# Twelve of 56 gate-times-up products move from VectorE to GpSimd in a fused S4-convolution and gated-MLP kernel

## The chip, the cores and the metric

The kernel runs on one core of one Trainium2 chip. The metric is device time in microseconds (us) of that core. In the profile PE is TensorE (PEld its weight loads), DVE is VectorE, ACT is ScalarE, POOL is GpSimd and SP is SyncE. SBUF is the on-chip working memory, PSUM the memory into which matmuls accumulate. bf16 is the type of almost all data; matmuls accumulate in f32.

## The reference

Input `A_u` has 2048 tokens of 512 features. It is layer-normalised, and three things are summed:

```python
x  = A_u
xn = _layernorm(x)
return x + A(xn, ...) + B(xn, w_gate, w_up, w_down)

# A: a diagonal state-space (S4) layer with 128 modes: a kernel K of length 2048 per feature is
#    built from powers of exp(dt*A), the tokens are convolved with it, and xn*Dskip is added
# B: g = xn @ w_gate; u = xn @ w_up        (512 -> 1792)
#    h = sigmoid(g) * u
#    return h @ w_down                     (1792 -> 512)
```

The change touches only `h = sigmoid(g) * u`.

## The kernel before

**B, the gated MLP.** The 2048 tokens go in four groups of 512, the 1792 hidden features in 14 tiles of 128. Group `grp` and tile `k` make a unit, `un = 14*grp + k`, of 56. A unit is four matmuls of 128x512 for the gate (line 1031), four for up (line 1055), a sigmoid on ACT from PSUM into a slot of `hT_sb` in SBUF (line 1043, or 1046 for two units at once), and a product `hT = hT * up`, in place, on DVE (line 1070). The units in the list `UEV` (36 of 56) have their up result first copied by ACT from PSUM to one of the two slots of `us_sb` (line 1066), and the product then reads two SBUF operands. The other 20 products read up from PSUM. When the 14 products of a group are done, 4 x 14 matmuls with `w_down` follow (line 1099). For groups 0 to 2 their result goes to `glu_sb` and GpSimd issues a DMA that adds x to it (line 1136, six of them); the final sum is made on DVE at the end (line 1010).

**A, the convolution.** DVE squares a complex factor again and again (lines 679 and 681) and builds tables of powers, in four chunks of features, by complex multiplications of four `tensor_tensor` each (lines 737, 738, 742, 743) and by squarings that begin on ACT (line 790) and end on DVE (lines 795, 796). Matmuls turn the tables into the kernel K (lines 821, 841, 914). The tokens are transformed by matmuls (698, 892), multiplied with K's transform on DVE (919, 923) and transformed back (936, 995).

**GpSimd** has little: the `pow` of the layernorms (lines 482, 483, 499), two memsets of a table's first column per chunk (770, 771), a few prefix sums of four elements (712 to 716), the six DMAs of line 1136, and some memsets at the start.

**What sets the order.** Every step is registered with `pl.add(engine, cost, function, ...)`, with the slots that it takes (`acq`) and gives back (`rel`). A list written out in the file, `ORDER`, says in which order the steps are emitted; slots are handed out first-in-first-out in that same order. The costs and priorities of `pl.add` play no part while `ORDER` is there. Each engine runs its own instructions strictly in the order of emission and waits by semaphores on others. So the next copy into a `us_sb` slot (line 1066 on ACT) waits until the product that reads the slot is done, and the down matmuls wait for the products of their group.

Of the kernel before, what the change touches and what calls it, by code (L numbers as in the profile page):

```python
# [14 lines left out]
ALU = mybir.AluOpType  # L15
# [39 lines left out]
PPROD = 23.23  # L55
# [125 lines left out]
def _consts():  # L181
# [22 lines left out]
UEV = (3, 5, 8, 9, 10, 11, 15, 16, 17, 18, 19, 20, 21, 23, 24, 26, 27, 28, 29, 30, 31, 32, 33, 34, 35, 36, 37, 38, 39, 40, 41, 42, 43, 44, 45, 54)  # L204
ON_DVE = (64, 67, 73, 76, 97, 98, 110, 121, 122, 123, 124, 482, 836, 838)
ON_ACT = (2,)
ORDER = [
# [52 lines left out]
class _Plan:  # L260
# [32 lines left out]
    def run(self):  # L293

        for n in ORDER or range(len(self.ops)):
            op = self.ops[n]
# [24 lines left out]
def kernel(  # L321
# [12 lines left out]
    V, S, T, P, Y = nc.vector, nc.scalar, nc.tensor, nc.gpsimd, nc.sync  # L334
# [8 lines left out]
    pl = _Plan(dict(s=NS, gu=NGU, hT=NHT, zs=4, zx=2, xx=3, es=3, kb=2, pp=2, pq=2, vs=2, ot=3, tg=2, us=2, sq=2))  # L343
# [3 lines left out]
    def bank(slot, r=0):  # L347
        if slot.pool == "s":
            return pairs[slot.idx][:, 512 * r:512 * r + 512]
        return banks[slot.idx][:]  # L350

    def two(slot):
        return pairs[slot.idx][:]
# [14 lines left out]
    us_sb = const.tile([128, 2, 512], BF, name="us_sb")  # L368
# [85 lines left out]
    def w_at(w, cut, kt, k):  # L454
        n = max(n for n in range(len(cut) - 1) if cut[n] <= 128 * k)
        o = KT * cut[n] + kt * (cut[n + 1] - cut[n]) + 128 * k - cut[n]
        return w[:, o:o + 128]
# [19 lines left out]
    def ln_small(t0, t1, deps, prio):  # L477
# [7 lines left out]
        if t1 <= LN_ACT:  # L485
            def fv_():
                for i in range(t0, t1):
                    if i in ON_ACT:
                        V.scalar_tensor_tensor(out=stats[:, i % 4, 0:1], in0=mv[:, i, 0:1], scalar=-1.0, in1=mv[:, i, 0:1], op0=ALU.mult,
# [5 lines left out]
            def fw_():  # L495
                V.tensor_copy(out=q["m_f"], in_=mvb[:, s, 0])
            o_v = pl.add("DVE", 0.17 + 0.53 * len(set(range(t0, t1)) & set(ON_ACT)), fv_, deps, prio)
            o_w = pl.add("DVE", 0.14, fw_, [o_v], prio)
# [37 lines left out]
    def layernorm(i0, i1, prio):  # L536
        st = []
        for i in range(i0, i1):
            if i in ON_ACT:
                def fn(i=i):  # L540
                    S.activation(out=glu_sb[:, 7, :], in_=xn[:, i, :], func=ACT.Identity, scale=1.0 / D, accum_out=mv[:, i, 0:1])
                    S.activation(out=glu_sb[:, 7, :], in_=xn[:, i, :], func=ACT.Square, scale=float(D ** -0.5), accum_out=mv[:, i, 1:2])
# [206 lines left out]
    for c in range(4):  # L749
# [62 lines left out]
        for half_ in range(2):  # L812
            sl = _Slot("s")
# [63 lines left out]
    for p in range(NP):  # L877
        dsl = slice(DW * p, DW * p + DW)
        for u in UNITS[p]:
# [6 lines left out]
            sl = _Slot("s")  # L886
# [128 lines left out]
    for grp in range(4):  # L1015
        hts, prods = [], []
        for u2 in range(7):
            hs = _Slot("hT")
            hts.append(hs)
            evs = []  # L1020
            joint = grp == 0 and u2 in JOINT
            for k in (2 * u2, 2 * u2 + 1):
                a, b = _Slot("s" if joint else "gu"), _Slot("gu")
                if joint and k % 2:
                    a = a0
                a0 = a
                GP = 80 + grp + k * 0.01

                def fg(k=k, sl=a, w=wg_sb, grp=grp, c0=0, c1=512):
                    for kt in range(KT):  # L1030
                        T.matmul(bank(sl, k % 2)[:, c0:c1], w_at(w, CUT_G, kt, k), xnT[:, grp, kt, c0:c1], start=(kt == 0),  # L1031
                                 stop=(kt == KT - 1))
                if joint:
                    mg = pl.add("PE", 0.864, fg, xnT_ready[grp] + [l_wg[piece(k)]] + ([mg] if k % 2 else []), 80 + k * 0.001,
                                acq=[] if k % 2 else [a])
                elif grp == 0 and k < 3:
                    mg = pl.add("PE", 0.44, lambda fg=fg: fg(c1=256), [xnT_ready[0][0], l_wg[0]], 60 + k * 0.001, acq=[a])
                    mg = pl.add("PE", 0.44, lambda fg=fg: fg(c0=256), [xnT_ready[0][1], mg], 70 + k * 0.001)
                else:
                    mg = pl.add("PE", 0.864, fg, xnT_ready[grp] + [l_wg[piece(k)]], 80 + k * 0.001 if grp == 0 else GP, acq=[a])  # L1040

                def fs(k=k, sl=a, hs=hs):
                    S.activation(out=hT_sb[:, hs.idx, k % 2, :], in_=bank(sl), func=ACT.Sigmoid)  # L1043

                def fs2(sl=a, hs=hs):
                    S.activation(out=hT_sb[:, hs.idx, :, :].rearrange("p k n -> p (k n)"), in_=two(sl), func=ACT.Sigmoid)
                if joint:
                    es_ = pl.add("ACT", 0.90, fs2, [mg], PSIG, tab="sig", acq=[hs], rel=[a]) if k % 2 else None
                else:
                    es_ = pl.add("ACT", 0.48, fs, [mg] + evs[-1:], PSIG, tab="sig", acq=[hs] if k % 2 == 0 else [], rel=[a])  # L1050
                evs.append(es_)

                def fu(k=k, sl=b, grp=grp):
                    for kt in range(KT):
                        T.matmul(bank(sl), w_at(wu_sb, CUT_U, kt, k), xnT[:, grp, kt, :], start=(kt == 0),  # L1055
                                 stop=(kt == KT - 1))
                mu = pl.add("PE", 0.864, fu, xnT_ready[grp] + [l_wu[k // 7]], GP + 0.005, acq=[b])

                h = lambda hs=hs, k=k: hT_sb[:, hs.idx, k % 2, :]
                un = FT * grp + k  # L1060
                us = _Slot("us")
                on = un in UEV

                def feu(sl=b, us=us, on=on):
                    if on:
                        S.activation(out=us_sb[:, us.idx, :], in_=bank(sl), func=ACT.Identity)  # L1066
                eu = pl.add("ACT", 0.48, feu, [mu], PSIG, acq=[us] if on else [], rel=[b] if on else [], alt=(un, 1))

                def fpd(sl=b, h=h, us=us, on=on):
                    V.tensor_tensor(out=h(), in0=h(), in1=us_sb[:, us.idx, :] if on else bank(sl), op=ALU.mult)  # L1070
                tail = dict(rel=[us] if on else [b], alt=(un, 2))
                if joint and k % 2 == 0:
                    held = fpd, [eu, mu], tail
                    continue
                if joint:
                    prods.append(pl.add("DVE", 0.33, held[0], held[1] + [es_], PPROD, **held[2]))
                prods.append(pl.add("DVE", 0.33, fpd, [es_, eu, mu], PPROD, **tail))
        ges = []
        for jj in range(4):
            i = grp * 4 + jj  # L1080
# [114 lines left out]
```

## Time and profile before

| | |
|---|---|
| median of 3 runs | 223.22 us (221.82 to 225.51) |
| span of the profiled execution, first to last instruction | 219.8 us |
| what the median has around that span | 3.4 us |
| mean granted TensorE clock | 0.999 |
| products from SBUF on DVE (line 1070) | 36, shortest 394, median 424, longest 438 ns |
| products from PSUM on DVE (line 1070) | 20, shortest 656, median 684, longest 700 ns |
| copies of up to SBUF on ACT (line 1066) | 36, median 616 ns |
| GpSimd's longest group | line 714, 3 instructions, 6.1 us |

A duration of DVE or ACT in the profile overlaps the next instruction's by some 0.1 us; what an instruction takes from its engine is the time from its start to the next start. Lines are those of the kernel before. The two profiles' line numbers differ after line 206.

### The profile page before, as it was taken

Reading aid. Unit: us, or ns where it says so; the run is one execution under the profiler, and the core shown is the slowest. Engines: PE = TensorE matmul, PEld = TensorE weight load, DVE = VectorE, ACT = ScalarE, POOL = GpSimd, SP = SyncE. Lnnn points to the kernel's source line nnn. Section 1 sums busy time; section 2 is a strip of 40 time slices with the busy share of each in tenths; the row PEclk is TensorE's granted clock in tenths of the full one; section 3 lists DMA queues with packets and bytes.
Section 4 is the critical chain, followed back from the end, with each engine's and each line's share of the span. In section 5 each row is a group of like instructions: output and inputs, shape, how many; then the busy total and the mean of one; then the engine's idle time right before and its main releaser. Section 6 shows DMA issues by size and latency. Waiting matters only on the chain.

```text
span 219.8 us, 5357 instructions
## 1 busy us (share of the span) xinstructions
PE 209.2 (95%) x2075; PEld 105.0 (48%) x2103; DVE 202.2 (92%) x444; ACT 175.9 (80%) x283; POOL 22.6 (10%) x39
## 2 busy tenths in 40 slices
PE   7999988999999999999999999999989999999994
PEld 2544433444434454445555555554555455543453
DVE  3999999999999999999999999999989999993582
ACT  3699999999999999769899999977578978942000
POOL 2216001001000049100000004000020100000000
PEclk9999999999999999999999999999999999999999
DMA  5997069216667064526818579856857987688743
GB/s 172 333 425 298 7 180 317 80 42 143 237 134 206 18 198 97 202 82 178 244 55 237 152 244 210 212 173 169 228 111 236 265 265 232 189 234 209 220 158 136
DMA packets 40651, 41.36 MB, mean 188 GB/s; under 512 B 9009, under 2 KB 31922, under 8 KB 40498
## 3 DMA queue, kind: packets, MB, share of 16 engines
q1 hardware_dynamic: 39458, 39.12, 57.7%
q0 software_dynamic: 864, 1.57, 4.9%
q10 hardware_dynamic: 304, 0.33, 0.6%
q8 instruction: 16, 0.26, 0.5%
q14 instruction: 9, 0.07, 0.1%
HBM read 25.28 MB, written 12.06 MB: 170 GB/s over the span
## 4 chain that ended last, share of the span: by engine, by line
DVE 48%; PE 41%; DMA 4%; ACT 4%; issue 2%; POOL 0%; DVEq 0%; ACTq 0%
PE bank L1099 11%; DVE big L738 7%; PE pair L914 7%; DVE big L737 6%; PE bank L1031 6%; PE bank L1055 6%; DVE hT_sb L1070 6%; PE pair L936 5%; DVE stats L547 4%; DVE big L742 4%; DVE big L743 3%; DVE big L679 3%; DVE big L681 3%; DMA big<-c_E 3%; ACT big L290 3%; DVE big L613 2%
## 5 line engine op out<-in xcount | busy, mean ns | idle before, releaser
L290 ACT ACTIVATE big<-pair 128x1024 bf16<-128x1024 f32 (+2 forms) x75 | 73.4, 996 | 9.2 <-PE pair L936 1.9
L1055 PE MATMUL bank<-xnT,wu_sb 128*128 128x512 bf16 x214 | 54.4, 379 | 2.5 <-ACT us_sb L1066 1.3
L1031 PE MATMUL bank<-xnT,wg_sb 128*128 128x512 bf16 (+1 forms) x211 | 50.9, 367 | 1.4 <-ACT xnT L576 0.4
L1099 PE MATMUL bank<-wd_sb,hT_sb 128*128 128x512 bf16 (+1 forms) x230 | 50.2, 366 | 0.4
L1043 ACT ACTIVATE hT_sb<-bank 128x512 bf16<-128x512 f32 x52 | 32.1, 643 | 3.8 <-PE bank L1031 3.6
L1031 PEld LDWEIGHTS <-wg_sb 128*128 128x128 bf16 x236 | 21.9, 98 | 26.4 <-issue 5.2
L1099 PEld LDWEIGHTS <-hT_sb 128*128 128x128 bf16 x238 | 22.5, 98 | 24.8 <-issue 2.1
L1055 PEld LDWEIGHTS <-wu_sb 128*128 128x128 bf16 x224 | 21.0, 97 | 27.2 <-issue 5.4
L737 DVE TENSOR_TENSOR big<-big 128x1024 bf16<-128x1024 bf16 (+4 forms) x40 | 26.8, 670 | 0.1
L738 DVE TENSOR_TENSOR big<-big 128x1024 bf16<-128x1024 bf16 (+4 forms) x40 | 26.6, 666 | 0.0
L1066 ACT ACTIVATE us_sb<-bank 128x512 bf16<-128x512 f32 x36 | 22.4, 634 | 0.0
L919 DVE TENSOR_TENSOR big<-big 128x2048 bf16<-128x2048 bf16 x16 | 19.5, 1219 | 0.4
L914 PE MATMUL pair<-big 128*128 128x256 bf16 x160 | 19.8, 272 | 0.1
L914 PEld LDWEIGHTS <-big 128*128 128x128 bf16 x160 | 15.5, 98 | 4.9 <-issue 1.1
L790 ACT ACTIVATE sq_sb<-big 128x256 bf16<-128x256 bf16 (+2 forms) x20 | 13.7, 685 | 3.9 <-DVE big L743 3.8
L743 DVE TENSOR_TENSOR big<-big 128x512 bf16<-128x512 bf16 (+4 forms) x40 | 16.6, 414 | 0.0
L742 DVE TENSOR_TENSOR big<-big 128x512 bf16<-128x512 bf16 (+4 forms) x40 | 16.5, 413 | 0.0
L290 ACT ACTIVATE big<-big 128x256 bf16<-128x256 bf16 x36 | 15.7, 470 | 0.2
L1070 DVE TENSOR_TENSOR hT_sb<-hT_sb,us_sb 128x512 bf16<-128x512 bf16 x36 | 14.9, 421 | 0.0
L905 DVE COPY big<-big 32x1024 bf16<-32x1024 bf16 x32 | 13.5, 421 | 0.5
L1070 DVE TENSOR_TENSOR hT_sb<-hT_sb,bank 128x512 bf16<-128x512 bf16 x20 | 13.2, 684 | 0.5 <-PE bank L1055 0.5
L936 PE MATMUL pair<-big 64*64 64x512 bf16 (+1 forms) x256 | 12.8, 326 | 0.5 <-ACT big L290 0.2
(103 smaller groups left out, 222.2 us busy)
## 6 DMA issues: line engine op xcount, KB each, us to landing
big<-c_E SPq DMA_DIRECT2D x16, 320.0 KB, 4.4
z_scr<-big SPq DMA_DIRECT2D x16, 256.0 KB, 3.0
big<-z_scr SPq DMA_DIRECT2D x16, 256.0 KB, 3.5
v_scr<-big SPq DMA_DIRECT2D x16, 256.0 KB, 2.9
big<-in_A_u_dram SPq DMA_DIRECT2D x4, 512.0 KB, 8.5
big<-big SPq DMA_DIRECT2D x32, 64.0 KB, 3.1
big<-v_scr SPq DMA_DIRECT2D x4, 512.0 KB, 5.0
wu_sb<-in_B_w_up_dram SPq DMA_DIRECT2D x2, 896.0 KB
```

The source lines that it names most:

```text
L290: nc.scalar.activation(out=get(out), in_=get(in_), func=ACT.Identity)
L737: V.tensor_tensor(out=wide(outp), in0=wide(lo), in1=mre, op=ALU.mult)
L738: V.tensor_tensor(out=wide(tb()), in0=wide(lo), in1=mim, op=ALU.mult)
L742: V.tensor_tensor(out=outp[:, :, 0], in0=outp[:, :, 0], in1=tb()[:, :, 1], op=opr)
L743: V.tensor_tensor(out=outp[:, :, 1], in0=outp[:, :, 1], in1=tb()[:, :, 0], op=opi)
L914: T.matmul(two(sk)[:, o:o + DW], es()[:, g, kt, :], kT[p][:, kt, :], start=kt in (0, NKT - 1), stop=kt >= NKT - 2)
L936: T.matmul(two(sv)[o:o + 64, DW * (2 * g + y):2 * DW * (g + 1)], mab[b:b + 64, 2 * u + g, q, :], pq()[b:b + 64, q, ch] if y else pp()[b:b ...
L1031: T.matmul(bank(sl, k % 2)[:, c0:c1], w_at(w, CUT_G, kt, k), xnT[:, grp, kt, c0:c1], start=(kt == 0), stop=(kt == KT - 1))
L1043: S.activation(out=hT_sb[:, hs.idx, k % 2, :], in_=bank(sl), func=ACT.Sigmoid)
L1055: T.matmul(bank(sl), w_at(wu_sb, CUT_U, kt, k), xnT[:, grp, kt, :], start=(kt == 0), stop=(kt == KT - 1))
L1070: V.tensor_tensor(out=h(), in0=h(), in1=us_sb[:, us.idx, :] if on else bank(sl), op=ALU.mult)
L1099: T.matmul(bank(po)[:, 0:c[1] - c[0]], hT_sb[:, hts[k // 2].idx, k % 2, jj * 128:(jj + 1) * 128], wd_sb[:, k, c[0]:c[1]], start=first and ...
```

## The change

A new list names twelve units, all of them in `UEV`: one of group 0, seven of group 1, four of group 2. Their product is issued on GpSimd (`P`) and not on DVE (`V`). The copy of up to `us_sb` stays as it was, and `ORDER` is the same list, so PE, ACT and SP have the same instructions in the same order. DVE's sequence has the twelve products taken out. GpSimd's has them put in at the place where `ORDER` emits them. Of the waits, those that waited on DVE for one of the twelve products now wait on GpSimd.

```diff
 ON_ACT = (2,)
+ON_POOL = (11, 15, 16, 19, 20, 21, 23, 24, 28, 30, 32, 34)
...
-                on = un in UEV
+                pool = un in ON_POOL
+                on = un in UEV or pool
...
-                    V.tensor_tensor(out=h(), in0=h(), in1=us_sb[:, us.idx, :] if on else bank(sl), op=ALU.mult)
+                    (P if pool else V).tensor_tensor(out=h(), in0=h(), in1=us_sb[:, us.idx, :] if on else bank(sl), op=ALU.mult)
...
-                prods.append(pl.add("DVE", 0.33, fpd, [es_, eu, mu], PPROD, **tail))
+                prods.append(pl.add("POOL" if pool else "DVE", 1.4 if pool else 0.33, fpd, [es_, eu, mu], PPROD, **tail))
```

GpSimd's sequence after the third layernorm's `pow` (line 483) is now: products of units 11, 20, 23, 15; the first DMA of line 1136; products 24, 16, 21, 19; memsets (770, 771); the second DMA; the prefix sums (712 to 716); products 34, 30; memsets; products 28, 32; memsets; the other DMAs and line 861.

More of the change, by code (lines that the diff above doesn't have):

```diff
@@ L1067, with fpd @@
                 eu = pl.add("ACT", 0.48, feu, [mu], PSIG, acq=[us] if on else [], rel=[b] if on else [], alt=(un, 1))
-                def fpd(sl=b, h=h, us=us, on=on):
-                    V.tensor_tensor(out=h(), in0=h(), in1=us_sb[:, us.idx, :] if on else bank(sl), op=ALU.mult)
+                def fpd(sl=b, h=h, us=us, on=on, pool=pool):
+                    (P if pool else V).tensor_tensor(out=h(), in0=h(), in1=us_sb[:, us.idx, :] if on else bank(sl), op=ALU.mult)
                 tail = dict(rel=[us] if on else [b], alt=(un, 2))
```

## The prediction

> **What bounds the kernel now.** First the page, busy times and the slices over the span, then the chain that ended last:
>
> ```profile
> PE 209.2 (95%) x2075; PEld 105.0 (48%) x2103; DVE 202.2 (92%) x444; ACT 175.9 (80%) x283; POOL 22.6 (10%) x39
> ...
> PE   7999988999999999999999999999989999999994
> ...
> DVE  3999999999999999999999999999989999993582
> ACT  3699999999999999769899999977578978942000
> POOL 2216001001000049100000004000020100000000
> ...
> DVE 48%; PE 41%; DMA 4%; ACT 4%; issue 2%; POOL 0%; DVEq 0%; ACTq 0%
> ```
>
> PE and DVE are both full, and POOL looks free. Busy PE could hide slack, so I looked at its starts in the timeline: matmuls of 512 columns start 0.216 us apart through all of the middle, while the granted clock is 1.00. PE is full in fact. The windows view over the stretch that holds the products says how much a faster DVE could give:
>
> ```profile
> 40.00:200.00 160.00, 156.85 (x1788) 80.28 (x1811) 157.08 (x344) 140.83 (x225) 14.74 (x19) 1.00 0.63 176
> ```
>
> The columns are the length, then busy PE, PEld, DVE, ACT, POOL. PE is idle for 160.00 - 156.85 = 3.15 us there. Its order is fixed, so nothing that DVE gives up after 40 us can bring more than that. The other direction is open: in the ten-us windows from 40 to 150 DVE is busy 9.90 us or more, and the chain of waits stays on DVE without a break to about 108 us. Lost DVE time there has no reserve to go into.
>
> **What leaves DVE.** The groups view with shapes kept apart has the two kinds of product:
>
> ```profile
> L1070 DVE TENSOR_TENSOR hT_sb<-hT_sb,us_sb 128x512 bf16<-128x512 bf16 x36 | 14.9, 421 | 0.0
> ...
> L1070 DVE TENSOR_TENSOR hT_sb<-hT_sb,bank 128x512 bf16<-128x512 bf16 x20 | 13.2, 684 | 0.5 <-PE bank L1055 0.5
> ```
>
> All twelve are of the first kind. One starts at 79.22 and its follower at 79.56 in the timeline, another at 33.61 and 33.95: 0.338 us from start to start. DVE is relieved of 12 x 0.338 = 4.06 us.
>
> **What one product takes on GpSimd.** No row shows one. The nearest rows, from the timeline of POOL:
>
> ```profile
> 0.85 0.52 POOL L519 MEMSET glu_sb<- 128x512 bf16 x1
> ...
> 81.24 0.22 POOL L714 TENSOR_TENSOR pre<-pre,xnT 128x4 f32<-128x4 f32 x1
> ```
>
> The memset writes 512 elements per partition in 0.52 us; memsets of one element take 0.10. That is 0.42 us for a pass over 512 elements. A two-operand operation on nearly nothing costs 0.22. If both operands and the result pass side by side, the product takes 0.22 + 0.42 = 0.65; if one after another, 0.22 + 3 x 0.42 = 1.50. I take two passes for two operands, the write hidden: 0.22 + 2 x 0.43 = 1.08 us, the middle of the two ends.
>
> **Does GpSimd's latency hurt by itself?** I matched the copies of line 1066, the sigmoids and the products in the timeline to their units. On DVE a product starts up to 4 us after its inputs are there, since it queues. On GpSimd it starts when the copy ends. Inputs are ready at (us): unit 11 38.05; 20 57.45; 23 62.30; 15 66.26; 24 70.98; 16 74.20; 21 76.21; 19 79.64; 34 106.00; 30 110.82; 28 113.20; 32 127.93. The next copy into the same `us_sb` slot started at 42.45, 65.48, 68.33, 70.34, 73.53, 78.48, 78.98, 82.52, 112.56, 113.94, 117.92, 128.72. With 0.06 for the hand-over and 1.08 for the product, each is done 1.4 to 6.9 us ahead of that copy, but for unit 32, which is 0.35 late. The first down matmuls that need a moved product start at 43.69 (unit 11), 83.37 to 84.23 (15, 16, 19) and 139.0 (28, 32), all 2.7 us or more behind. Alone, then, the latency costs nothing until a product takes 1.08 + 1.4 = 2.5 us.
>
> What is queued behind the products on POOL waits longer: the first DMA of line 1136 goes from 50.32 to about 67.4 (unit 15), but its sum is read on DVE at 200 us; the memsets at 101.87 go to about 112 (unit 30), and the matmuls that read them run from 131.19; the prefix sums feed work near 196 us. These cost nothing. The third layernorm's `pow` stands ahead of unit 11 and keeps its place. No queue of SP or ACT is passed.
>
> **What GpSimd does to DVE.** This is the term that decides. DVE instructions that read two SBUF tensors fill its time: from 55 to 83 us all but three products from PSUM and one line-560 instruction, from 105 to 130 all but one of line 852. There is one place where GpSimd reads SBUF against that:
>
> ```profile
> 82.07 5.44 POOL L714 TENSOR_TENSOR pre<-pre,xnT 128x4 f32<-128x4 f32 x1
> ...
> 82.04 0.43 DVE L1070 TENSOR_TENSOR hT_sb<-hT_sb,us_sb 128x512 bf16<-128x512 bf16 x1
> 82.38 0.47 DVE L737 TENSOR_TENSOR big<-big 128x512 bf16<-128x512 bf16 x1
> ...
> 87.04 0.39 DVE L796 TENSOR_TENSOR big<-big 128x384 bf16<-128x384 bf16 x1
> 87.54 1.09 DVE L737 TENSOR_TENSOR big<-big 128x1792 bf16<-128x1792 bf16 x1
> ```
>
> The same four-element operation that took 0.22 takes 5.44 here. It spans 13 two-operand DVE instructions without a gap and ends 0.07 us after the last of them, in the first gap of DVE. So the two do not read side by side. What DVE pays when GpSimd is in first can't be seen with four elements; the `pow` of line 483, in flight from 19.08 to 20.41, did not hold a two-operand instruction that started at 19.79 (line 679, its usual 0.69), but its four elements were surely read by then. Bounds: DVE pays nothing, or it stands for as long as the product reads, its whole 1.08. I take the second, as a product of 512 elements reads nearly to its end.
>
> [...]
>
> The sum: I laid the 1.08 us of each product over DVE's rows at its ready time, leaving out instructions with one SBUF operand and the moved product itself. Nine products meet two-operand work for all of it, 9 x 1.08 = 9.72; unit 11 for 0.37, unit 23 for 0.89, unit 32 for 0.76. Together 11.74. Less the relief: 11.74 - 4.06 = **+7.7 us**. DVE is full at all of these places, so I let all of it reach the end: span 219.8 + 7.7 = 227.5, and with the 3.4 us around the span 223.2 + 7.7 = **230.9**. With 0.65 a product it is 0.65 / 1.08 x 11.74 - 4.06 = +3.0 (226.2), with 1.50 it is +12.2 (235.4).
>
> **The rivals.**
>
> *GpSimd reads beside DVE at no cost to it* (not slower). For it: the `pow` row, and the slack of every product. Against it: the 5.44. DVE gains 4.06, but PE's idle time of 3.15 is the ceiling, and the waits of PE on named engines after 38 us add up to 0.6. I take 0.7: **222.5**. It decides if DVE's two-operand instructions keep their spacing next to a product.
>
> *DVE always goes first* and GpSimd starves, as in the 5.44 row. A product then waits for the next one-operand DVE instruction or gap. By the rows, units 24, 16, 21, 19, 30, 28 and 32 would wait longer than their slack (unit 19: next such instruction at 97.59, copy at 82.52). The copy on ACT stands, ACT's queue with it, until DVE runs out of ACT's results; then GpSimd gets in. Each costs DVE a hole of one product, the held copy and the next ACT instruction: 1.08 + 0.63 + 0.47 = 2.2 us. 7 x 2.2 - 4.06 = +11.2: **234.4**; the same with 0.65 and 1.50 gives 231 and 237. It decides from a product latency of 2.5 us.
>
> *DVE pays half*, because the reads go in turns: 5.87 - 4.06 = +1.8, **225.0**.
>
> **How the numbers follow.** Forecast 0.48, starving GpSimd 0.20, half price 0.13, no cost 0.17, and 0.02 for a gain that the PE ceiling does not allow. Two per cent of 223.2, about what a measurement here tells from no change, is 4.5 us, so the bounds are 218.8 and 227.7. Slower takes starvation and the forecast but for its low end: 0.20 + 0.46 = 0.66. Within: 0.02 + 0.13 + 0.17 = 0.32. Faster: 0.02. The range goes from 223, just above the case of no cost, to 236.5, which leaves out the dearest end of starvation.
>
> **What would show it.** Twelve POOL rows of line 1070's product with 1.0 to 1.2 us each, and next to each a gap of DVE, or a stretched two-operand instruction, of up to the same length; DVE idle some 8 us more between 55 and 130 where it had none; PE idle the same; POOL in the chain of waits. Products of 3 us and more, with ACT idle before line 1066's copies, would show starvation. Unbroken DVE rows at 0.34 us spacing next to products of about 1 us would show the forecast wrong.

## The result and the profile after

The changed kernel takes 229.92 us (median of 4 runs, 229.67 to 232.51); the kernel before took 222.52 us beside it (median of 4). It is slower by 7.4 us, ratio 1.0379, 95% interval 1.0321 to 1.0437. The profiled execution has a span of 228.1 us against 219.8, at a granted clock of 0.997.

The page of the changed kernel: busy times, three rows of the slices, and the chain that ended last.

```profile
PE 213.2 (93%) x2103; PEld 105.5 (46%) x2103; DVE 207.4 (91%) x432; ACT 176.3 (77%) x283; POOL 44.0 (19%) x51
...
PE   7989979999999789999988999999989999999993
...
ACT  3799999899999598769798969977579978942000
POOL 1215013100784383000550043000020100000000
...
PE 42%; DVE 35%; DMA 12%; ACT 3%; issue 3%; SPq 3%; DVEq 0%; ACTq 0%
```

DVE has twelve instructions fewer and is busy 5.2 us longer. PE and ACT have slices of 7 and 5 where they had 9, above the slices in which POOL is now busy. In the chain DMA has 12% where it had 4%; 8.9 us of that are a load that starts at 4.5 us, ahead of every moved product, and the write-only run below, which loses nothing, has the same load in its chain. The view of waits shows what PE and ACT stood for (in total, times, longest; PE's wait for these copies was 1.3 us in 3 before):

```profile
PE bank L1056 <- ACT us_sb L1068: 3.4, 4, 1.4
...
ACT us_sb L1068 <- DVE hT_sb L1072: 2.3, 1, 2.3
ACT us_sb L1068 <- POOL hT_sb L1072: 2.2, 2, 1.7
```

The view of the product's own line shows what became of the twelve (durations in ns: shortest, median, longest; then first and last start in us):

```profile
L1072 POOL TENSOR_TENSOR hT_sb<-hT_sb,us_sb x12: 1144/1680/6947, 38.3 to 134.0; 128x512 bf16<-128x512 bf16 x12
```

The shortest, 1.14 us, I take to be the product by itself; three of the twelve took 1.14 to 1.19. The others waited inside their row. How, the timelines of POOL and DVE show at two places (start, duration). Unit 15:

```profile
67.14 1.42 POOL L1072 TENSOR_TENSOR hT_sb<-hT_sb,us_sb 128x512 bf16<-128x512 bf16 x1 [0.61 <-ACT us_sb L1068]
...
66.85 0.69 DVE L738 TENSOR_TENSOR big<-big 128x1024 bf16<-128x1024 bf16 x1
67.46 1.64 DVE L739 TENSOR_TENSOR big<-big 128x1024 bf16<-128x1024 bf16 x1
```

Unit 20:

```profile
58.34 6.95 POOL L1072 TENSOR_TENSOR hT_sb<-hT_sb,us_sb 128x512 bf16<-128x512 bf16 x1 [17.56 <-ACT hT_sb L1044]
...
57.76 0.68 DVE L682 TENSOR_TENSOR big<-big 128x512 f32<-128x512 f32 x1
58.36 1.08 DVE L738 TENSOR_TENSOR big<-big 128x1792 bf16<-128x1792 bf16 x1
...
63.59 0.68 DVE L682 TENSOR_TENSOR big<-big 128x512 f32<-128x512 f32 x1
64.19 0.68 DVE L1072 TENSOR_TENSOR hT_sb<-hT_sb,bank 128x512 bf16<-128x512 bf16 x1
64.78 0.72 DVE L796 TENSOR_TENSOR big<-sq_sb 128x384 bf16<-128x384 bf16 x1
```

Unit 15 gets in at the end of a DVE instruction, and the next one (line 739) takes 1.64 us where its equal takes 0.69: DVE is *held* 0.96 us. Unit 20 gets in nowhere between 58.34 and 64.19, while DVE keeps its full pace; then comes a DVE product that reads PSUM, and the GpSimd product is done 1.10 us after that one's start. GpSimd *starves*. At its end it holds DVE too, but only the last part of it meets a two-operand instruction: line 796 is 0.37 us longer than usual.

To add up, I took DVE's stretch from the last `bn_aggr` of the third layernorm (line 548 before) to the last multiplication of line 923, and gave each instruction the median start-to-start spacing of its line and shape in the kernel before ("work"). Time in which DVE had no instruction is "idle". What a spacing has beyond work and idle is "held" where it is over 0.2 us, and "rest" otherwise. In us:

| run | stretch | work | held | idle | rest | ratio to before |
|---|---|---|---|---|---|---|
| before | 160.93 | 158.68 | 0 | 1.88 | 0.36 | 1 |
| changed | 168.05 | 154.66 | 8.80 | 3.96 | 0.62 | 1.0379 |
| products left out | 160.36 | 154.66 | 0 | 4.37 | 1.32 | 0.9966 |
| write only | 160.54 | 154.66 | 0.69 | 3.96 | 1.22 | 0.9987 |
| extra reads | 172.61 | 158.68 | 10.22 | 3.25 | 0.45 | 1.0510 |
| one operand | 164.44 | 158.68 | 3.91 | 1.52 | 0.33 | 1.0149 |
| seven | 169.11 | 156.34 | 4.09 | 7.98 | 0.70 | 1.0385 |
| unit 24 alone | 167.03 | 158.35 | 0 | 8.00 | 0.69 | 1.0265 |
| unit 11 alone | 160.77 | 158.35 | 0.89 | 1.21 | 0.32 | 0.9999 |

The change: -4.02 of work, +8.80 held, +2.08 idle, +0.26 rest make +7.12 us. Of the 8.3 us between the two profiled spans, the other 1.2 lie ahead of the stretch (0.4) and behind it (0.8). Eleven of the twelve hold DVE: six of them (units 15, 16, 19, 23, 28, 30) by 0.96 to 1.06 us, the other five by 0.25 to 0.89. Unit 32 holds nothing: DVE stands idle 1.68 us, up to 137.17, for a copy on ACT that had waited 1.75 us for this product. The idle column by itself does not show starving, though: it is as high in the two runs in which nothing starves and DVE, relieved, runs ahead of ACT (left out, write only).

### The profile page after: what moved, and what is told of

Read it like the earlier page. It is cut to its first block, busy times and chain, and to the rows that moved or that the text cites. A ratio compares the mean times of both kernels' runs of the same rounds, so it can differ in the third digit from the quotient of the medians.

```text
span 228.1 us, 5383 instructions
## 1 busy us (share of the span) xinstructions
PE 213.2 (93%) x2103; PEld 105.5 (46%) x2103; DVE 207.4 (91%) x432; ACT 176.3 (77%) x283; POOL 44.0 (19%) x51
## 4 chain that ended last, share of the span: by engine, by line
PE 42%; DVE 35%; DMA 12%; ACT 3%; issue 3%; SPq 3%; DVEq 0%; ACTq 0%
PE bank L1101 15%; PE bank L1032 7%; PE pair L915 6%; DVE big L739 5%; DVE hT_sb L1072 4%; PE bank L1056 4%; DMA big<-in_A_u_dram 4%; PE pair L937 4%; DVE big L738 3%; SPq L424 3%; DVE big L682 3%; DVE big L680 3%; DMA big<-c_E 3%; DVE stats L548 2%; ACT big L291 2%
## 5 line engine op out<-in xcount | busy, mean ns | idle before, releaser
L1056 PE MATMUL bank<-xnT,wu_sb 128*128 128x512 bf16 x224 | 55.1, 379 | 5.1 <-ACT us_sb L1068 3.4
L1032 PE MATMUL bank<-xnT,wg_sb 128*128 128x512 bf16 (+1 forms) x220 | 52.0, 368 | 1.3 <-DVE hT_sb L1072 0.5
L1101 PE MATMUL bank<-wd_sb,hT_sb 128*128 128x512 bf16 (+1 forms) x238 | 50.8, 367 | 0.2 <-ACT us_sb L1068 0.2
L1072 POOL TENSOR_TENSOR hT_sb<-hT_sb,us_sb 128x512 bf16<-128x512 bf16 x12 | 27.6, 2304 | 70.2 <-ACT us_sb L1068 52.6
L1044 ACT ACTIVATE hT_sb<-bank 128x512 bf16<-128x512 f32 x52 | 31.3, 626 | 3.8 <-PE bank L1032 3.8
L739 DVE TENSOR_TENSOR big<-big 128x1024 bf16<-128x1024 bf16 (+4 forms) x40 | 29.2, 731 | 0.0
L738 DVE TENSOR_TENSOR big<-big 128x1024 bf16<-128x1024 bf16 (+4 forms) x40 | 26.5, 664 | 0.3
L920 DVE TENSOR_TENSOR big<-big 128x2048 bf16<-128x2048 bf16 x16 | 20.5, 1278 | 0.4
L744 DVE TENSOR_TENSOR big<-big 128x512 bf16<-128x512 bf16 (+4 forms) x40 | 17.2, 431 | 0.0
L743 DVE TENSOR_TENSOR big<-big 128x512 bf16<-128x512 bf16 (+4 forms) x40 | 17.1, 427 | 0.1
L548 DVE BATCH_NORM_STATS2 stats<-big 128x6 f32<-128x512 bf16 x15 | 10.2, 677 | 3.5 <-DMA big<-in_A_u_dram 3.5
```

Of the source, the lines that this page charges most:

```text
L738: V.tensor_tensor(out=wide(outp), in0=wide(lo), in1=mre, op=ALU.mult)
L739: V.tensor_tensor(out=wide(tb()), in0=wide(lo), in1=mim, op=ALU.mult)
L920: V.tensor_tensor(out=pp().rearrange("p q h m -> p (q h) m"), in0=xx().rearrange("p q h m -> p (q h) m"), in1=kb()[:, 0:2 * DW].unsqueeze( ...
L1072: (P if pool else V).tensor_tensor(out=h(), in0=h(), in1=us_sb[:, us.idx, :] if on else bank(sl), op=ALU.mult)
L1101: T.matmul(bank(po)[:, 0:c[1] - c[0]], hT_sb[:, hts[k // 2].idx, k % 2, jj * 128:(jj + 1) * 128], wd_sb[:, k, c[0]:c[1]], start=first and ...
```

## The experiments

Diffs are against the changed kernel and shortened. Most of them replace the one product line of the function `fpd`, which is not repeated each time; `us_sb[...]` stands for `us_sb[:, us.idx, :]`. Each time is a median; behind it stand the ratio to the kernel before, run beside it, and the ratio's 95% interval.

**Products left out.** The kernel leaves the twelve products out: the relief alone.

```diff
-(P if pool else V).tensor_tensor(out=h(), in0=h(), in1=us_sb[...] if on else bank(sl), op=ALU.mult)
+if not pool:
+    V.tensor_tensor(out=h(), in0=h(), in1=us_sb[...] if on else bank(sl), op=ALU.mult)
```

> The twelve products are left out altogether: neither VectorE nor GpSimd computes them, all else as in the changed kernel. This is the relief alone. My theory (VectorE stands while GpSimd reads): VectorE gives up 4.06 us, TensorE had 3.15 us of idle time from 40 to 200 us, so the time is 0 to 3 us under the kernel before, likeliest 0.7 us (ratio 0.987 to 1.000). A rival by which the relief itself is worth its full 4.06 us gives 0.982.

221.58 us, before 222.32; ratio 0.9966 (0.9940 to 0.9992). As expected: taking 4.02 us of work from DVE is worth 0.7 us; DVE's idle time takes up 2.5 of it.

**Write only.** The kernel leaves the twelve products out, and GpSimd overwrites both tiles with zeros.

```diff
+if pool:
+    for _ in range(2):
+        P.memset(us_sb[:, us.idx, :], 0.0)
+        P.memset(h(), 0.0)
+    return
```

> In place of each of the twelve products GpSimd writes four memsets of 128x512, in turn into the us_sb slot and into the hT tile (the product is not computed). Everything waits for GpSimd as in the changed kernel, and it is occupied some 2 us per unit, but it reads nothing. My theory: no VectorE instruction is stretched; the ratio to the kernel before is 0.99 to 1.005. The rival, that the loss comes from GpSimd's latency through the us_sb slots and from its queue, gives nearly the ratio of the changed kernel, 1.03 to 1.04, since 2 us is about the median duration of a product there (1.68 us).

221.85 us; 0.9987 (0.9959 to 1.0016), as expected. The timelines of POOL and DVE at unit 24:

```profile
72.15 0.52 POOL L1075 MEMSET hT_sb<- 128x512 bf16 x1
72.62 0.51 POOL L1074 MEMSET us_sb<- 128x512 bf16 x1
...
71.93 1.22 DVE L739 TENSOR_TENSOR big<-big 128x2048 bf16<-128x2048 bf16 x1
73.07 0.29 DVE L796 TENSOR_TENSOR big<-sq_sb 128x256 bf16<-128x256 bf16 x1
```

GpSimd is occupied for four memsets of 0.52 us per unit, the same instructions of ACT and PE depend on it as in the changed kernel, and the run takes only 0.3 us more than the one in which the products are left out. In the stretch two casts (line 665) are held, 0.7 us together, and no `tensor_tensor`. GpSimd's first DMA of line 1136 goes out at 68.85 us, as late as in the changed kernel (68.50; 50.32 before). So the loss is not GpSimd's queue nor a latency of 2 us; it needs reading.

**Extra reads.** DVE makes all products; GpSimd multiplies twelve tiles once more, by a piece of `wu_sb` that only serves as something to read.

```diff
+V.tensor_tensor(out=h(), in0=h(), in1=us_sb[...] if on else bank(sl), op=ALU.mult)
+if pool:
+    P.tensor_tensor(out=h(), in0=h(), in1=wu_sb[:, 0:512], op=ALU.mult)
```

> VectorE keeps all 56 products as in the kernel before. After each of the twelve, GpSimd multiplies the same hT tile in place by a 128x512 piece of wu_sb: an addition, so the hidden features of these units come out changed. No us_sb slot waits for GpSimd; only the down matmuls do, and they come 2.7 us or more later. My theory: VectorE loses about 0.96 us to each (what the rows of the changed kernel show) and is not relieved, 12 x 0.96 = 11.5 us, so 9 to 12 us over the kernel before (ratio 1.040 to 1.054). The latency rival: nobody waits for GpSimd, ratio 1.00 to 1.005.

233.36 us; 1.0510 (1.0469 to 1.0550), 11.0 us more, as expected. Held 10.22 us, in twelve places. One of the twelve starved longest of all, from the timelines of POOL and DVE:

```profile
117.20 18.21 POOL L1074 TENSOR_TENSOR hT_sb<-hT_sb,wu_sb 128x512 bf16<-128x512 bf16 x1 [23.84 <-DVE hT_sb L1072]
...
134.13 0.27 DVE L744 TENSOR_TENSOR big<-big 128x256 bf16<-128x256 bf16 x1
134.35 1.34 DVE L1072 TENSOR_TENSOR hT_sb<-hT_sb,us_sb 128x512 bf16<-128x512 bf16 x1
```

From 117.20 to 134.35 DVE ran two-operand instructions only, 37 of them without a gap, and lost nothing. Then it was held all the same: its product at 134.35 takes 1.34 us, 0.93 more than usual. The 17 us of waiting cost nothing by themselves, as no `us_sb` slot waited for this instruction; they did not spare DVE the hold.

**One operand.** DVE makes all products; GpSimd copies twelve tiles onto themselves.

```diff
+V.tensor_tensor(out=h(), in0=h(), in1=us_sb[...] if on else bank(sl), op=ALU.mult)
+if pool:
+    P.tensor_copy(out=h(), in_=h())
```

> As the run with twelve extra multiplications (VectorE keeps all products), but GpSimd's extra instruction has one SBUF operand: it copies the hT tile of 128x512 onto itself. My theory: VectorE stands for the time in which GpSimd reads, and one operand is half of the reading, so 12 x 0.5 = 6 us over the kernel before, half of the 11.4 us of the two-operand run (ratio 1.020 to 1.032). If only GpSimd instructions with two operands hold VectorE: 1.00. If the hold goes with the instruction and not with what it reads: 1.045 or more.

225.65 us; 1.0149 (1.0116 to 1.0182), below the range expected. The shortest copy takes 0.62 us, and none holds DVE for more than 0.41 us, against 0.96 for two operands. That the price goes with the reading stands; one operand costs 3.6 us, less than half of the 11.0 that two cost.

**Own slots.** Rows 6 and 7 of `glu_sb` as slots for the eight early units.

```diff
-us = _Slot("us")
+us = _Slot("ux" if un in ON_POOL and un < 28 else "us")
...
```

> The changed kernel, but the eight moved units of groups 0 and 1 copy up into two slots of their own (rows 6 and 7 of glu_sb, not in use until later), so that the copies of the other units don't wait for GpSimd. My theory: the holds of VectorE (some 10 us) stay, only ACT's waits go (2.3 and 0.45 us before line 1068 up to 83 us), so the time falls by 0 to 2 us from the changed kernel (ratio to the kernel before 1.025 to 1.038). The latency rival: most of the loss goes, ratio 1.01 or less.

231.69 us; 1.0432 (1.0400 to 1.0464): slower, a miss of both accounts. The eight units now share two slots among themselves. Unit 24 took 8.15 us and a copy on ACT waited 3.54 for it; held time fell to 7.31, and DVE's idle time rose to 7.25. The run does not separate the two accounts; it shows that starving has a price where a slot is wanted.

**Seven of the twelve**, those that had taken under 2 us.

```diff
-ON_POOL = (11, 15, 16, 19, 20, 21, 23, 24, 28, 30, 32, 34)
+ON_POOL = (15, 16, 19, 23, 24, 28, 30)
```

> Seven of the twelve stay on GpSimd (units 15, 16, 19, 23, 24, 28, 30: those whose product took under 2 us in the changed kernel); units 11, 20, 21, 32 and 34, which took 2.4 to 7 us there, go back to VectorE. My theory, that the price is a hold of 0.96 us for each product less 0.34 us of relief, gives 7 x 0.62 = 4.3 us (ratio 1.015 to 1.025). If the price came from the five starved products, hardly anything would be left, ratio 1.00 to 1.007.

230.55 us; 1.0385 (1.0358 to 1.0411): as dear as the twelve, against both accounts. Held time is halved to 4.09, but unit 24, 1.14 us long in the changed kernel, takes 8.33 us here and ACT stands 5.72 us before a copy. In the changed kernel it starts at 71.87, beside a DVE product that reads PSUM (71.59 to 72.26); here it starts at 71.03, and DVE runs two-operand instructions without a gap to 78.35. Which product starves thus depends on what DVE runs at the moment, and the other moved products shift that.

**Half on each engine.** Columns 0 to 255 on GpSimd, the rest on DVE.

```diff
+if pool:
+    for e, c in ((P, slice(0, 256)), (V, slice(256, 512))):
+        e.tensor_tensor(out=h()[:, c], in0=h()[:, c], in1=us_sb[:, us.idx, c], op=ALU.mult)
+    return
```

> All twelve moved products are cut in two: columns 0 to 255 on GpSimd, 256 to 511 on VectorE. My theory: the hold is in proportion to the elements, 12 x 0.5 = 6.0 us, and the relief 12 x (0.34 - 0.20) = 1.7 us, so 4.3 us over the kernel before (ratio 1.012 to 1.024). A fixed price for each GpSimd instruction would give 12 x 0.96 - 1.7 = 9.8 us, ratio 1.044.

229.89 us; 1.0345 (1.0315 to 1.0375), a miss. Each hold is 0.5 us at most, as expected, 3.47 together. But the halves of units 20 and 24 take 6.48 and 7.25 us, a copy on ACT waits 4.65 us, and DVE idles 7.57 in the stretch.

**Five late ones.**

```diff
+ON_POOL = (42, 43, 44, 45, 54)
```

> Five other products go to GpSimd in place of the twelve: units 42, 43, 44, 45 and 54, whose products stand between 142 and 197 us in the kernel before, four of them after 170 us, where VectorE has idle time (0.2 to 1.1 us in each 10 us from 160) and TensorE sets the pace. My theory: the holds, 5 x 0.62 = 3.1 us net, are partly taken up there, so 0 to 2.5 us over the kernel before (ratio 1.000 to 1.011). If every hold reaches the end: 1.014. If lateness at the end is what counts, units 43 and 45 delay the down matmuls of the last group, 1.01 and more with TensorE waiting on GpSimd.

226.07 us; 1.0178 (1.0147 to 1.0209), a miss: 4.0 us for five. From the timelines of DVE and POOL:

```profile
177.01 3.05 DVE L906 COPY big<-big 32x1024 bf16<-32x1024 bf16 x4
...
193.24 3.50 DVE L906 COPY big<-big 32x1024 bf16<-32x1024 bf16 x4
...
177.96 0.83 POOL L862 MEMSET big<- 128x512 bf16 x1
```

Four of these copies take 1.71 us in the kernel before. Held 4.96 us in six places. Two are two-operand instructions (0.86 and 1.04 us). Four are copies of line 906, which have one SBUF operand (0.25, 1.06, 0.91 and 0.85 us); the one of 1.06, at 177.70, stands beside GpSimd's memset and DMA issues, when no product is left. DVE's stretch is 4.9 us longer than before: its little idle time there did not take the holds up.

**One product alone**, after seven had cost as much as twelve.

```diff
+ON_POOL = (24,)
```

and the same with `(11,)`.

> Unit 24 alone on GpSimd. In the kernel before its inputs are ready at 70.98, VectorE has two-operand instructions from there to 78.6, and the next copy into the slot is at 73.53. If a starved product is what costs (it held ACT 5.7 us in the run with seven), 2.5 to 6 us over the kernel before (ratio 1.011 to 1.027). If each product costs its hold alone, 0.62 us, ratio 1.000 to 1.005.

> Unit 11 alone on GpSimd. Its slack to the next copy into the slot is 3.3 us, and one-operand casts of line 664 stand next to it, so nothing starves by either account: the hold of 0.9 us less 0.34 of relief, 0 to 0.6 us over the kernel before, ratio 0.999 to 1.004. If moving any product cost the same, a twelfth of the change's 7.4 us, 0.6 us, would also be 1.003: what tells is this run beside unit 24's.

Unit 24 alone: 228.04 us, 1.0265 (1.0236 to 1.0295): one product costs 6.0 us, where the twelve of the change cost 7.4. Unit 11 alone: 222.04 us, 0.9999 (0.9981 to 1.0016). Both as expected. Unit 24 in the timelines of POOL, ACT, DVE and PE, and in the windows (length, busy PE, PEld, DVE, ACT, POOL with their counts, granted clock, DMA):

```profile
70.95 7.64 POOL L1072 TENSOR_TENSOR hT_sb<-hT_sb,us_sb 128x512 bf16<-128x512 bf16 x1 [19.68 <-ACT us_sb L1068]
```

```profile
72.92 0.68 ACT L1044 ACTIVATE hT_sb<-bank 128x512 bf16<-128x512 f32 x1
78.63 0.60 ACT L1068 ACTIVATE us_sb<-bank 128x512 bf16<-128x512 f32 x1 [5.03 <-POOL hT_sb L1072]
```

```profile
77.29 0.29 DVE L744 TENSOR_TENSOR big<-big 128x256 bf16<-128x256 bf16 x1
79.26 0.43 DVE L1072 TENSOR_TENSOR hT_sb<-hT_sb,us_sb 128x512 bf16<-128x512 bf16 x1 [1.67 <-ACT us_sb L1068]
```

```profile
74.05 1.03 PE L1056 MATMUL bank<-xnT,wu_sb 128*128 128x512 bf16 x4
79.28 1.86 PE L1056 MATMUL bank<-xnT,wu_sb 128*128 128x512 bf16 x4 [4.21 <-ACT us_sb L1068]
```

```profile
74.00:78.60 4.60, 1.07 (x5) 0.39 (x4) 3.59 (x10) 0.00 (x0) 4.59 (x1) 0.87 0.00 0
78.60:84.00 5.40, 4.72 (x12) 1.57 (x11) 1.45 (x3) 5.06 (x9) 0.00 (x0) 0.50 0.06 20
```

DVE is not held at all. It runs on until 77.58, then has nothing that ACT had not to deliver first; the product gets in there and is done at 78.59, 1.0 us later. ACT stood 5.03 us for the slot, PE 4.21 us for ACT, and for the 5.4 us after that PE's granted clock is 0.50: four matmuls take 1.86 us where they took 1.03. An estimate from these figures: 4.21 us of standing and half of 5.4 at the lower clock are 6.9 us of PE's time, of which 6.0 reached the end.

Unit 11 took 2.42 us. From DVE's timeline:

```profile
38.56 0.76 DVE L665 CAST big<-big 128x512 bf16<-128x512 f32 x2
...
39.41 1.19 DVE L744 TENSOR_TENSOR big<-big 128x128 bf16<-128x128 bf16 x1
```

Its product was ready at 38.05. The two casts, which read one operand, pass before it, and line 744 is held 0.89 us. The hold less 0.33 of relief was taken up by DVE's idle time, which is 0.67 lower than before. No slot waited.

**What lets GpSimd in.** A one-element DVE copy in each complex multiplication, in the changed kernel and in the kernel before.

```diff
 V.tensor_tensor(out=wide(outp), in0=wide(lo), in1=mre, op=ALU.mult)
+V.tensor_copy(out=k2[:, 0:1], in_=one[:])
 V.tensor_tensor(out=wide(tb()), in0=wide(lo), in1=mim, op=ALU.mult)
```

> The changed kernel with a VectorE copy of one element (one SBUF operand, into a scratch column that is overwritten later) between the two multiplications of each complex multiplication, 40 in all. Theory: GpSimd's product gets in as soon as VectorE runs an instruction with one SBUF operand or stands idle. Then no product lasts over 2.5 us (in the changed kernel five did, up to 7 us), ACT's waits ahead of line 1068 go, and each of the twelve is a hold of 0.96 us: 12 x 0.96 - 4.06 = 7.5 us and the price of the copies, some 40 x 0.07 = 2.8 us, ratio to the kernel before 1.040 to 1.052. Rival: an instruction as short as this lets nothing in, products of 3 to 7 us stay.

> The kernel before with the same 40 copies of one element: the price of the copies by itself. 40 x 0.07 us (the spacing of the shortest VectorE rows) = 2.8 us or less, ratio 1.005 to 1.015.

With the change 231.39 us, 1.0417 (1.0384 to 1.0449); without it 224.69, 1.0117 (1.0090 to 1.0143); both as expected. Unit 20 in the timelines of POOL and DVE:

```profile
58.15 2.25 POOL L1073 TENSOR_TENSOR hT_sb<-hT_sb,us_sb 128x512 bf16<-128x512 bf16 x1 [17.73 <-ACT hT_sb L1045]
...
59.27 0.18 DVE L739 COPY k<-one 128x1 f32<-128x1 f32 x1
59.33 2.02 DVE L740 TENSOR_TENSOR big<-big 128x1792 bf16<-128x1792 bf16 x1
```

It gets in after the first short copy and holds line 740 by 0.94 us; in the changed kernel it took 6.95 us. The longest product is 2.60 us, a little over the 2.5 expected, so the short copies do let GpSimd in. ACT still waits 1.49 us for a late DVE product and 1.21 for a moved one, which was not expected. Held time is 10.80 in twelve places, idle time the same in both (2.16 and 2.15). Between the two kernels, 231.39 - 224.69 = 6.7 us, and 10.80 held less 4.02 of relief is 6.8. In these two runs, where no product starves for long, holds less relief are the whole price.

## Why the prediction was right, and where it was not

Forecast +7.7 and 230.9 us; measured +7.4 and 229.92. The sign and the cause (reading, not latency or the queue) hold. The size is in part luck: two terms were off, in opposite directions.

*The ceiling and the relief.* 4.06 us forecast, 4.02 in the table; by itself worth 0.7 forecast, 0.7 measured.

*The product's time.* 1.08 taken between 0.65 and 1.50; the shortest is 1.14. The value taken was the middle of two bounds, and no row told which of them was nearer.

*DVE stands for the whole reading.* Nearly: 0.96 us for a full hold, of a product of 1.14. In the write-only run 48 memsets held no `tensor_tensor`. That a product gets in when it is ready and DVE then stands fits unit 15 (0.96 us) and not unit 20, before which ten DVE instructions passed in 5.85 us, none of them held.

*The sum of 11.74 us* was too large: the table has 8.80. I had let each product in at its ready time, for all of its reading at nine places. Six holds came out in full. Five of the twelve products (units 11, 20, 21, 32, 34) took 2.45 to 6.95 us since DVE went first, and got in partly beside a DVE instruction that reads PSUM (units 20, 21 and 34 were done 1.08 to 1.10 us after the start of one) or in a hole of DVE (unit 32, 1.68 us). That a DVE instruction with one SBUF operand stands outside all this, as the sum takes it, is shown by no run: the two casts beside unit 11 passed (0.76 us for both) before its product got in, but two casts lost 0.7 us beside memsets (write only), and four copies of line 906 lost 0.25 to 1.06 us each (five late ones).

*"The latency costs nothing until a product takes 2.5 us"* was true as a condition and wrong as a forecast, since products did take that long. ACT waited 1.75 us (unit 32) and 0.45 us for moved products, 2.31 for a late DVE product, and DVE's idle time rose by 2.08. I had this as a rival to the forecast, "DVE always goes first"; in fact both happen in one run. 8.80 + 2.08 is 10.88 against 11.74: that a term which I put at nothing made up for most of what the other had too much is luck.

*The signs.* Three products of 1.14 to 1.19 us and the stretched instructions came as foretold; so did two products of over 3 us, the sign of starving. DVE was not idle 8 us more between 55 and 130, but 0.2: the holds lie inside its rows. PE's idle time there rose by 3.1 us, not 8, and POOL is not in the chain.

*The time.* The 3.4 us around the span set a median of three runs against one profiled execution; in every later run an execution has 1.7 to 2.3 us around its own span. So the difference, +7.7, is what can be held against the result, and 230.9 less so.

*The rivals.* No cost is refuted by the extra reads; half price by the 0.96. The rival of the starving product has the right mechanism for five of the twelve, but named seven units of which two starved (21 and 32). Its price of 2.2 us for each was too low for unit 24 alone, which cost 6.0: neither the 4.21 us of PE's standing nor the clock after it was in that price. It was too high for unit 11, which cost nothing alone. And its condition, "the next one-operand DVE instruction or gap", is too wide: the casts did not let unit 11 in.

What stays open: at some ends of a two-operand DVE instruction GpSimd gets in (unit 15), at others it does not (unit 20 stood through ten of them, the extra read through 37 and then got in at such an end). The one-element copies show a way in; they don't tell what decides between two `tensor_tensor`. Each kernel has one profile, so the runs don't show either whether the same product starves in every execution.

## What to carry to other kernels

An elementwise instruction with two SBUF operands that is moved from a full VectorE to GpSimd may not leave VectorE: here the 0.34 us of relief of each was mostly paid for with a hold (0.96 us in full), or with a wait of ACT and TensorE for a starved product (5.03 and 4.21 us for unit 24 alone). Before moving work off a busy engine, leave the work out once: here that showed that all there was to gain was 0.7 us. And the price of one moved instruction cannot be multiplied: one alone cost nothing, another 6 us, seven 8.5 and twelve 7.4.

## What the runs showed of the hardware

In the run with extra reads a stream of 37 two-operand VectorE instructions without a gap kept a GpSimd product of 1.1 us waiting for 17 us (row of 18.2 us) and lost nothing until the product got in. In the changed kernel a full hold was 0.96 to 1.06 us, for 128x512 with two operands; in the run with one operand a hold was 0.41 at most. The 48 memsets of that size held no `tensor_tensor`, but two casts (f32 to bf16, 0.7 us together). With five late products four of VectorE's copies of 32x1024 from SBUF to SBUF were held too, by 0.25 to 1.06 us, the longest beside a memset and DMA issues. A one-element VectorE copy let a waiting product in (2.25 us in place of 6.95). With unit 24 alone TensorE stood 4.21 us; in the 5.4 us after that its granted clock was 0.50, four matmuls took 1.86 us where they had taken 1.03, and the run lost 6.0 us. In the changed kernel, with shorter stalls (1.4 us at most for these copies), the clock was 1.00 from 70 to 90 us.
